# Windowed attention followed by a phase mixer: all x tiles of later batches turned by DMA, theta products split around a channel product

## The chip, the cores and the metric

The kernel runs on one core of a Trainium2 chip. The metric is device time in microseconds (us) of one execution. Five engines with queues of their own work at once: TensorE (PE, matmuls; its weight loads are listed apart as PEld), VectorE (DVE), ScalarE (ACT), GpSimd (POOL) and SyncE (SP, which here only issues DMAs). Each engine takes its instructions in the order in which they were written.

## The reference

Two stages follow each other, for 4 batches, 8 heads, 768 positions and heads of 64 channels (512 channels together).

```
scores = q @ k.T / 8 - slope[h] * dist     # only the 8 first and the 96 last positions are kept
x      = softmax(scores) @ v               # heads side by side: 768 x 512
theta  = x @ w_theta
y      = w_tok_r @ (x * cos(theta)) + w_tok_i @ (x * sin(theta))
u      = x + y
out    = u + max(u @ w_ch, 0)
```

## The kernel before

Positions are cut into six tiles of 128 (`st` or `tt`), channels into four blocks of 128 (`dc`). Heads are worked in pairs, so that a pair's output is one block of 128 channels: pair 0 gives x's channels 0 to 127, pair 3 the last 128.

**Attention of a pair** (`att_transpose`, `att_scores`, `att_values`): q and k are turned on PE into PSUM tiles `ps_tr` (L215) and copied out (L225); scores go in three groups into a wide PSUM tile `ps_w` (L267), ACT takes the exponential (L276), DVE multiplies by a mask (L286, L288), PE multiplies by v into another `ps_w` (L315), and DVE divides by the sums and writes the pair's part of `x_sb` (L322, L323).

**Mixing of a batch**: theta needs x with channels on partitions, `xT`. `turn_x` makes one pair's part of it in one of two ways: six PE transposes into a `ps_tr` tile (L347) and a DVE copy (L352), or one transposing DMA from SBUF to SBUF, issued by SP (L341). `mix_theta(b, st)` then computes theta for two position tiles in one `ps_w` tile: 8 products of 128x128 by 128x512 (L364), after which ACT takes cosine and sine from it (L372, L373). `mix_z` multiplies these by x on DVE (L380, `zri`). `mix_tok` sums twelve products for a position tile in a PSUM tile `ps_mm` (L399), DVE adds x (L404, `u`), and SP issues a transposing DMA of u (L413, `uTd`). `mix_ch` multiplies that by `w_ch` in a `ps_mm` tile (4 products, L441), DVE finishes it (L444), and SP issues the store (L446).

**PSUM.** `ps_w` has two buffers, `ps_mm` two, `ps_tr` two. They are taken in turn, so the next but one user of a kind waits until the readers of the earlier one are done.

**Order.** It is written out by hand. `attend_beside(b + 1, ...)` interleaves attention of batch b + 1 with token products of batch b (`main`, a list of units, taken one or more at a time by `m()`). Then comes the stretch that is changed, in which batch b's last channel products stand between batch b + 1's theta products. It is passed three times, for b + 1 = 1, 2, 3; they are called batches 1, 2 and 3 here. `load` is true in batches 1 and 2, where heads of a further batch are fetched by POOL's DMAs meanwhile (L75, L80). With it, pairs 0 and 1 are turned by DMA, pair 2 on PE ahead of the last units of `main` (L492), pair 3 on PE after a channel product (L586). Batch 3 turns pairs 0, 1 and 2 by DMA and pair 3 on PE. So seven pairs go by DMA and five on PE. Batch 0 has its own order ahead of the loop (L500 to L570) and isn't touched.

In batches 1 and 2, `att_transpose` of the following batch puts its 24 PE transposes between `mix_theta(b + 1, 2)` and `mix_theta(b + 1, 4)`; its copies of k and q stand behind the sines of the latter on ACT and behind `mix_z(b + 1, 2)` on DVE.

Of the kernel before, what the change touches and what calls it, by code (L numbers as in the profile page):

```python
# [16 lines left out]
def kernel(  # L17
# [14 lines left out]
    B, H, S, D = q.shape  # L32
# [3 lines left out]
    NC = DM // T  # L36
# [19 lines left out]
    def ps_wide():  # L56
        return psum.tile([T, 2, DM], FP, name="ps_w", tag="ps_w", bufs=2)

    def ps_acc():
        return psum.tile([T, DM], FP, name="ps_mm", tag="ps_mm", bufs=2)  # L60

    def ps_tr(cols):
        return psum.tile([T, cols], BF, name="ps_tr", tag="ps_tr", bufs=2)
# [20 lines left out]
    def load_heads(b, h0, n):  # L84
        load_qk(b, h0, n)
        load_v(b, h0, n)
# [121 lines left out]
    def att_transpose(b, h0, extras=True, sins=None, q_eng="dve", between=None, cuts=(T,)):  # L208
        pq, pk = ps_tr(S), ps_tr(S)
        for src, pst in ((q_sb[b], pq), (k_sb[b], pk)):  # L210
            if pst is pk and between is not None:
                between()
            for t_ in range(NT):
                for hh in range(2):
                    K(nc.tensor.transpose(pst[hh * D:(hh + 1) * D, t_ * T:(t_ + 1) * T],  # L215
                                          src[:, h0 + hh, t_ * D:(t_ + 1) * D], ident))
        if sins is not None:
            sins()

        kT = abuf.tile([T, S + (NT - 2) * T], BF, name="kT", bufs=2)  # L220
        qT = abuf.tile([T, S], BF, name="qT", bufs=2)
        copy = nc.scalar.copy if q_eng == "act" else nc.vector.tensor_copy
        for op, dst, src in ((nc.scalar.copy, kT[:, 0:S], pk), (copy, qT, pq)):
            for p0, p1 in zip((0,) + cuts, cuts):
                K(op(out=dst.rearrange("a (p t) -> a p t", t=NT)[:, p0:p1, :],  # L225
                     in_=src.rearrange("a (t p) -> a p t", t=NT)[:, p0:p1, :]))
        qTs[b, h0], kTs[b, h0] = qT, kT
        if extras:
            att_extras(b, h0)
# [25 lines left out]
    def att_scores(b, h0, g_):  # L255
        qT, kT = qTs[b, h0], kTs[b, h0]
        blocks = GROUPS[g_]
        n = len(blocks)
        bias = b == 0
        if bias and (h0, g_) not in biased:  # L260
            att_bias(h0, g_)
        ps = biased[h0, g_] if bias else ps_wide()
        for i_, (it, prev) in enumerate(blocks):
            kc = it * T if prev == 0 else (0 if it == 1 else S + (it - 2) * T)
            for hh in range(2):
                R = slice(D * hh, D * (hh + 1))
                K(nc.tensor.matmul(ps[:, hh, i_ * T:(i_ + 1) * T],  # L267
                                   lhsT=kT[R, kc:kc + T], rhs=qT[R, it * T:(it + 1) * T],
                                   start=not bias, stop=not bias or i_ == n - 1))
        if bias:  # L270
            p = abuf.tile([T, 2, 4 * T], BF, name="p", bufs=6)
            K(nc.scalar.activation(p[:, :, 0:n * T], ps[:, :, 0:n * T], AF.Exp, scale=scale))  # L272
            probs[b, h0, g_] = p
            return
        e = abuf.tile([T, 2, 4 * T], BF, name="e", bufs=3)
        K(nc.scalar.activation(e[:, :, 0:n * T], ps[:, :, 0:n * T], AF.Exp, scale=scale))  # L276
        exps[b, h0, g_] = e
        att_mul(b, h0, g_)
# [58 lines left out]
    def turn_x(b, dc, by_dma, eng=nc.vector.tensor_copy):  # L337

        xT = xTs[b][:, dc, :]
        if by_dma:  # L340
            K(nc.sync.dma_start(out=xT.rearrange("a (c t) -> a c t", t=T),  # L341
                                in_=x_sb[b][:, dc, :, :].rearrange("a t d -> a (t d)"),
                                transpose=True))
            return
        pt = ps_tr(S)
        for st in range(NT):
            K(nc.tensor.transpose(pt[:, st * T:(st + 1) * T], x_sb[b][:, dc, st, :], ident))  # L347
        if eng == "both":
            K(nc.vector.tensor_copy(out=xT[:, 0:2 * T], in_=pt[:, 0:2 * T]))  # L349
            K(nc.scalar.copy(out=xT[:, 2 * T:], in_=pt[:, 2 * T:]))  # L350
        else:
            K(eng(out=xT, in_=pt))  # L352
# [3 lines left out]
    def mix_theta(b, st, d0=0, d1=NC):  # L356

        if d0 == 0:
            thetas[b, st] = ps_wide()
        pth = thetas[b, st]  # L360
        for s2 in range(2):
            for dc in range(d0, d1):
                c = (st + s2) * T
                K(nc.tensor.matmul(pth[:, s2, :], lhsT=xTs[b][:, dc, c:c + T],  # L364
                                   rhs=w_theta_bf[:, dc, :],
                                   start=(dc == 0), stop=(dc == NC - 1)))
        if d1 < NC:
            return
        if st == 0:
            zris[b] = mbuf.tile([T, NT, 2, DM], BF, name="zri", tag="zri", bufs=3)  # L370
        cs = mbuf.tile([T, 2, 2, DM], BF, name="cs", bufs=3)
        K(nc.scalar.activation(cs[:, :, 0, :], pth, AF.Sin, bias=halfpi))  # L372
        K(nc.scalar.activation(cs[:, :, 1, :], pth, AF.Sin))  # L373
        css[b, st] = cs

    def mix_z(b, st):
        cs = css[b, st]
        xs = x_sb[b][:, :, st:st + 2, :].rearrange("a c s d -> a s c d")
        for wi in range(2):
            K(nc.vector.tensor_mul(  # L380
                zris[b][:, st:st + 2, wi, :].rearrange("a s (c d) -> a s c d", d=T),
                cs[:, :, wi, :].rearrange("a s (c d) -> a s c d", d=T), xs))
# [49 lines left out]
    def mix_ch(b, tt, parts=1):  # L432
        uT, n, s2 = uTs[b, tt]
        out_t = out[b].rearrange("(t p) d -> p t d", p=T)[:, tt, :]
        N = DM // parts
        for part in range(parts):
            cols = slice(part * N, (part + 1) * N)
            pc = ps_acc()
            for dc in range(NC):
                c = (n * dc + s2) * T  # L440
                K(nc.tensor.matmul(pc[:, 0:N], lhsT=uT[:, c:c + T], rhs=w_ch_bf[:, dc, cols],  # L441
                                   start=(dc == 0), stop=(dc == NC - 1)))
            o_sb = mbuf.tile([T, N], FP, name="o_sb", bufs=4)
            K(nc.vector.scalar_tensor_tensor(o_sb, in0=pc[:, 0:N], scalar=0.0,  # L444
                                             in1=us[b][:, tt, cols], op0=ALU.max, op1=ALU.add))
            K(nc.sync.dma_start(out=out_t[:, cols], in_=o_sb))  # L446
# [24 lines left out]

    def attend_beside(b, main, lead, load):


        def m(n=1):
            for _ in range(n):
                main.pop(0)()

        m(lead)
        for h0 in range(0, H, 2):  # L480
            att_scores(b, h0, 0)
            m()
            att_scores(b, h0, 1)
            att_scores(b, h0, 2)
            if h0 + 2 < H:
                att_transpose(b, h0 + 2, q_eng="act")
                if load and h0 == 0:
                    load_heads(b + 1, 0, 4)
                m(2)
            else:  # L490
                if load:
                    turn_x(b, NC - 2, False)  # L492
                m(len(main) - 1)
            att_values(b, h0)
            if h0 + 2 < H and not (load and h0 + 4 == H):
                turn_x(b, h0 // 2, True)
            m()


# [72 lines left out]
    for b in range(B):  # L572
        if b == B - 1:
            main = tok_units(b, True)
            main.insert(-1, lambda: mix_uT(b, 4, 1, "act"))
            for unit in main:
                unit()
            mix_ch(b, 2)
            mix_ch(b, 3)
            mix_uT(b, 5, 1, "dve")  # L580
            mix_ch(b, 4)
            mix_ch(b, 5, parts=2)
            break
        attend_beside(b + 1, tok_units(b, b > 0), 3 if b else 0, b + 2 < B)
        mix_ch(b, 2)
        turn_x(b + 1, NC - 1, False)  # L586
        mix_ch(b, 3)
        mix_theta(b + 1, 0)
        mix_z(b + 1, 0)
        mix_ch(b, 4)  # L590
        mix_theta(b + 1, 2)
        mix_z(b + 1, 2)
        if b + 2 < B:
            att_transpose(b + 2, 0, sins=lambda: mix_theta(b + 1, 4))
            load_heads(b + 2, 4, 4)
        else:
            mix_theta(b + 1, 4)
        mix_ch(b, 5)
        mix_z(b + 1, 4)
# [35 lines left out]
```

## Time and profile before

| | us |
|---|---|
| median of 3 runs | 175.93 (175.57 to 175.95) |
| the profiled execution | 177.43 |
| its span, first to last instruction | 175.7 |
| what lies around the span | 1.73 |
| PE busy in the span | 165.6 |
| DVE busy | 111.7 |
| ACT busy | 103.8 |
| POOL busy | 60.6 |
| PE transposes of x (L347), 54 of them | 4.5 busy |
| xT by DMA (L341), 7 of them, issue to landing | 2.7 least, 7.1 median, 12.4 most |

Busy time says how long an engine had an instruction in it, and matmuls overlap, so that PE's own figure is not a sum of their lengths: a 128x512 product lasts 380 ns by itself, and eight behind each other take 1.73 us, so 0.216 us each. The timeline lists instructions by their start, with the length, and in brackets how long the engine had stood idle before it and who released it. A row that merges several instructions ("x8") gives the start of the first and the time to the end of the last.

### The profile page before, as it was taken

What the parts mean: (1) busy time and instruction counts of PE and PEld (TensorE: products, weight loads), DVE (VectorE), ACT (ScalarE), POOL (GpSimd) and SP (SyncE); (2) the same over time, 40 slices, a digit from 0 to 9 for tenths busy, and PEclk for the clock granted to TensorE, in tenths of its full rate; (3) what the DMA queues carried; (4) which work ended last, traced back from release to release, by engine and by line L of the source; (5) the groups of instructions that cost most, each with busy time, mean ns of one, the idle gap of its engine ahead of it and who ended that gap; (6) DMA issues with size and microseconds to landing.
All of it is one profiled execution on the core that took longest, in us unless ns stands there. A gap on an engine that the chain in (4) does not pass through costs nothing.

```text
span 175.7 us, 4158 instructions
## 1 busy us (share of the span) xinstructions
PE 165.6 (94%) x1740; PEld 88.1 (50%) x1740; DVE 111.7 (64%) x205; ACT 103.8 (59%) x121; POOL 60.6 (35%) x99
## 2 busy tenths in 40 slices
PE   7889999899999999999998979999999999999992
PEld 2346665566465554445454544546555544444441
DVE  7756654975768784857567691857568784734353
ACT  5697889947777553797846712797756807500010
POOL 8986695004571400049716100049118000000000
PEclk9999999999999999999999999999999999999999
DMA  5999999999999944117999996116999433312325
GB/s 150 185 174 191 212 207 209 191 189 177 131 142 161 193 84 149 63 60 92 174 98 180 153 147 208 63 60 90 174 93 160 104 97 118 119 30 60 90 109 189
DMA packets 57058, 24.05 MB, mean 137 GB/s; under 512 B 43088, under 2 KB 54096, under 8 KB 57040
## 3 DMA queue, kind: packets, MB, share of 16 engines
q0 software_dynamic: 35328, 12.45, 65.8%
q1 hardware_dynamic: 21440, 10.95, 32.0%
q10 hardware_dynamic: 272, 0.39, 0.6%
q8 instruction: 13, 0.21, 0.5%
q14 instruction: 5, 0.04, 0.1%
HBM read 25.69 MB, written 6.29 MB: 182 GB/s over the span
## 4 chain that ended last, share of the span: by engine, by line
PE 56%; DMA 20%; ACT 9%; DVE 7%; POOL 4%; issue 2%; ACTq 0%
PE ps_mm L399 21%; PE ps_mm L441 10%; PE ps_w L364 9%; DMA v_sb<-in_v_dram 7%; DMA uTd<-u 6%; PE ps_tr L215 4%; PE ps_w L267 4%; DMA k_sb<-in_k_dram 4%; PE ps_w L315 3%; ACT kT L225 3%; DMA first<-in_q_dram 3%; ACT cs L373 2%; DVE w_tokT L117 2%; PE ps_w L252 2%; PE ps_mm L315 2%
## 5 line engine op out<-in xcount | busy, mean ns | idle before, releaser
L399 PE MATMUL ps_mm<-zri,w_tokT 128*128 128x512 bf16 x288 | 69.8, 380 | 0.1
L276 ACT ACTIVATE e<-ps_w 128x1024 bf16<-128x1024 f32 (+1 forms) x36 | 33.0, 951 | 19.6 <-PE ps_w L267 19.6
L399 PEld LDWEIGHTS <-w_tokT 128*128 128x128 bf16 x288 | 25.7, 98 | 28.2 <-issue 0.6
L233 POOL COPY kT<-kT 128x512 bf16<-128x512 bf16 x15 | 9.3, 622 | 64.6 <-ACT kT L225 64.6
L372 ACT ACTIVATE cs<-ps_w,halfpi 128x1024 bf16<-128x1024 f32 x12 | 13.4, 1115 | 19.7 <-PE ps_w L364 19.6
L441 PE MATMUL ps_mm<-w_ch_bf,uTd 128*128 128x512 bf16 x88 | 22.6, 380 | 1.4 <-DMA uTd<-u 1.4
L364 PE MATMUL ps_w<-w_theta_bf,xT 128*128 128x512 bf16 x96 | 22.9, 380 | 0.6 <-DVE xT L349 0.4
L404 DVE TENSOR_TENSOR u<-x_sb,ps_mm 128x512 bf16<-128x512 bf16 x24 | 16.2, 681 | 10.5 <-PE ps_mm L399 10.5
L288 DVE TENSOR_TENSOR p<-e,wmask 128x1024 bf16<-128x1024 bf16 x24 | 17.4, 725 | 8.5 <-ACT e L276 8.4
L380 DVE TENSOR_TENSOR zri<-cs,x_sb 128x1024 bf16<-128x1024 bf16 x24 | 16.1, 687 | 9.1 <-ACT cs L372 7.7
L444 DVE SCALAR_TENSOR_TENSOR o_sb<-ps_mm,u 128x512 f32<-128x512 f32 (+1 forms) x25 | 16.6, 664 | 2.8 <-PE ps_mm L441 2.7
L267 PEld LDWEIGHTS <-kT 64*128 64x128 bf16 x352 | 10.0, 94 | 14.7 <-issue 11.0
L267 PE MATMUL ps_w<-qT,kT 64*128 64x128 bf16 x352 | 16.2, 218 | 0.5 <-DVE kT L234 0.5
L225 ACT COPY kT<-ps_tr 128x768 bf16<-128x768 bf16 (+2 forms) x17 | 12.9, 765 | 4.9 <-PE ps_tr L215 4.9
L315 PEld LDWEIGHTS <-p 128*128 128x128 bf16 x352 | 12.9, 97 | 4.5 <-issue 0.8
L364 PEld LDWEIGHTS <-xT 128*128 128x128 bf16 x96 | 8.9, 98 | 11.3 <-DVE xT L349 0.6
L441 PEld LDWEIGHTS <-uTd 128*128 128x128 bf16 x88 | 8.0, 98 | 10.4 <-DMA uTd<-u 1.5
L80 POOL DMA_DIRECT2D v_sb<-in_v_dram x10 | 13.0, 1305 | 0.0
L286 DVE TENSOR_TENSOR p<-e,wmask 128x768 bf16<-128x768 bf16 x12 | 6.7, 559 | 9.9 <-ACT e L276 9.9
L272 ACT ACTIVATE p<-ps_w 128x1024 bf16<-128x1024 f32 (+1 forms) x12 | 11.3, 953 | 1.7 <-PE ps_w L267 1.2
L373 ACT ACTIVATE cs<-ps_w 128x1024 bf16<-128x1024 f32 x12 | 12.2, 1020 | 0.0
L91 POOL COPY v_pv<-v_sb 128x520 bf16<-128x520 bf16 x15 | 9.3, 620 | 8.3 <-DMA v_sb<-in_v_dram 8.3
(80 smaller groups left out, 192.4 us busy)
## 6 DMA issues: line engine op xcount, KB each, us to landing
out_dram<-o_sb SPq DMA_DIRECT2D x23, 256.0 KB, 2.2
q_sb<-in_q_dram POOLq DMA_DIRECT2D x6, 384.0 KB, 8.5
k_sb<-in_k_dram POOLq DMA_DIRECT2D x6, 384.0 KB, 10.1
v_sb<-in_v_dram POOLq DMA_DIRECT2D x6, 384.0 KB, 13.8
w_nat<-in_moe_w_tok_r_dram POOLq DMA_DIRECT2D x1, 1152.0 KB, 12.2
w_nat<-in_moe_w_tok_i_dram POOLq DMA_DIRECT2D x1, 1152.0 KB, 13.4
v_sb<-in_v_dram POOLq DMA_DIRECT2D x4, 192.0 KB, 7.3
q_sb<-in_q_dram POOLq DMA_DIRECT2D x3, 192.0 KB, 6.8
```

Source lines behind the costliest of these rows:

```text
L225: K(op(out=dst.rearrange("a (p t) -> a p t", t=NT)[:, p0:p1, :], in_=src.rearrange("a (t p) -> a p t", t=NT)[:, p0:p1, :]))
L267: K(nc.tensor.matmul(ps[:, hh, i_ * T:(i_ + 1) * T], lhsT=kT[R, kc:kc + T], rhs=qT[R, it * T:(it + 1) * T], start=not bias, stop=not bias ...
L276: K(nc.scalar.activation(e[:, :, 0:n * T], ps[:, :, 0:n * T], AF.Exp, scale=scale))
L288: K(nc.vector.tensor_mul(p.rearrange("a h (r x) -> a h r x", r=2), e.rearrange("a h (r x) -> a h r x", r=2), wmask[:, hs, None, T:3 * T].t ...
L315: K(nc.tensor.matmul(dst, lhsT=lhsT, rhs=rhs, start=(i_ == 0), stop=(i_ == len(mms) - 1)))
L364: K(nc.tensor.matmul(pth[:, s2, :], lhsT=xTs[b][:, dc, c:c + T], rhs=w_theta_bf[:, dc, :], start=(dc == 0), stop=(dc == NC - 1)))
L373: K(nc.scalar.activation(cs[:, :, 1, :], pth, AF.Sin))
L380: K(nc.vector.tensor_mul(zris[b][:, st:st + 2, wi, :].rearrange("a s (c d) -> a s c d", d=T), cs[:, :, wi, :].rearrange("a s (c d) -> a s ...
L399: K(nc.tensor.matmul(acc, lhsT=w_tokT[wi][:, st, tt * T:(tt + 1) * T], rhs=zris[b][:, st, wi, :], start=(done[b, tt] == 0), stop=(done[b, ...
L404: K(nc.vector.tensor_add(us[b][:, tt, :].rearrange("a (c d) -> a c d", d=T), x_sb[b][:, :, tt, :], acc.rearrange("a (c d) -> a c d", d=T)))
L441: K(nc.tensor.matmul(pc[:, 0:N], lhsT=uT[:, c:c + T], rhs=w_ch_bf[:, dc, cols], start=(dc == 0), stop=(dc == NC - 1)))
L444: K(nc.vector.scalar_tensor_tensor(o_sb, in0=pc[:, 0:N], scalar=0.0, in1=us[b][:, tt, cols], op0=ALU.max, op1=ALU.add))
```

## The change

All pairs of batches 1, 2 and 3 are now turned by DMA, so five groups of six PE transposes and their DVE copies go, and five DMAs come, issued by SP straight after the pair's `att_values`. The products of theta are cut in two: for position tiles 0 to 3 those with the first three channel blocks come first (12 products in both `ps_w` tiles), then the channel product `mix_ch(b, 4)`, then the products with the last block (2 and 2), each followed by its sines.

```diff
@@ attend_beside
             else:
-                if load:
-                    turn_x(b, NC - 2, False)
                 m(len(main) - 1)
             att_values(b, h0)
-            if h0 + 2 < H and not (load and h0 + 4 == H):
-                turn_x(b, h0 // 2, True)
+            turn_x(b, h0 // 2, True)
             m()
@@ the loop over batches
         mix_ch(b, 2)
-        turn_x(b + 1, NC - 1, False)
         mix_ch(b, 3)
-        mix_theta(b + 1, 0)
+
+        mix_theta(b + 1, 0, 0, NC - 1)
+        mix_theta(b + 1, 2, 0, NC - 1)
+        mix_ch(b, 4)
+        mix_theta(b + 1, 0, NC - 1, NC)
         mix_z(b + 1, 0)
-        mix_ch(b, 4)
-        mix_theta(b + 1, 2)
+        mix_theta(b + 1, 2, NC - 1, NC)
         mix_z(b + 1, 2)
         if b + 2 < B:
             att_transpose(b + 2, 0, sins=lambda: mix_theta(b + 1, 4))
```

## The prediction

> **What bounds the kernel now.** First the page's busy shares and slices, then the chain of waits, then the timeline around the three stretches that change.
>
> ```profile
> PE 165.6 (94%) x1740; PEld 88.1 (50%) x1740; DVE 111.7 (64%) x205; ACT 103.8 (59%) x121; POOL 60.6 (35%) x99
> ...
> PEclk9999999999999999999999999999999999999999
> DMA  5999999999999944117999996116999433312325
> ```
>
> PE is the bound, at full clock throughout; the DMA engines are full (digit 9) through most of batch 2's attention, and nearly idle in the changed stretches of batches 1 and 3. So what PE loses counts, and so does what PE no longer has to do, but only where PE isn't waiting there anyway. I call the start of batch 1's first theta product T = 66.84; in batches 2 and 3 it is 106.57 and 143.45. Batch 1's stretch, from the timeline:
>
> ```profile
> 66.84 1.89 PE L364 MATMUL ps_w<-w_theta_bf,xT 128*128 128x512 bf16 x8
> 68.57 1.03 PE L441 MATMUL ps_mm<-w_ch_bf,uTd 128*128 128x512 bf16 x4
> 68.77 1.11 ACT L372 ACTIVATE cs<-ps_w,halfpi 128x1024 bf16<-128x1024 f32 x1 [4.81 <-PE ps_w L364]
> 69.78 1.02 ACT L373 ACTIVATE cs<-ps_w 128x1024 bf16<-128x1024 f32 x1
> 69.43 1.89 PE L364 MATMUL ps_w<-w_theta_bf,xT 128*128 128x512 bf16 x8
> 72.05 1.90 PE L364 MATMUL ps_w<-w_theta_bf,xT 128*128 128x512 bf16 x8
> ```
>
> Theta of tiles 0/1 is complete 1.89 us after T; its cosine starts 0.04 later and its sine ends at 70.80. The third theta tile (4/5) takes the buffer that these two read, and starts only at 72.05: 1.25 us to spare.
>
> **Removed: 30 PE transposes, 5 DVE copies.** Six transposes hold PE for 0.34 us (65.64 to 65.98 below), so five groups are 1.7 us at most. I find none of it on the path:
>
> ```profile
> 63.44 0.20 PE L315 MATMUL ps_w<-v_pv,p 128*128 128x65 bf16 x1 [0.16 <-DVE p L288]
> ...
> 65.25 0.68 DVE L404 TENSOR_TENSOR u<-x_sb,ps_mm 128x512 bf16<-128x512 bf16 x1
> 65.64 0.50 PE L347 MATMUL ps_tr<-ident,x_sb 128*128 128x128 bf16 x6
> 65.98 1.02 PE L441 MATMUL ps_mm<-w_ch_bf,uTd 128*128 128x512 bf16 x4
> ```
> ```profile
> 103.82 0.50 PE L347 MATMUL ps_tr<-ident,x_sb 128*128 128x128 bf16 x6
> ...
> 105.69 1.04 PE L441 MATMUL ps_mm<-w_ch_bf,uTd 128*128 128x512 bf16 x4 [1.37 <-DMA uTd<-u]
> ```
>
> - Pair 2, batch 1: PE already waits for the mask product p at 63.44. That ends at 63.38, behind scores that stand ahead of the removed group, so PE comes 0.34 earlier and waits 0.34 longer. Zero.
> - Pair 3, batches 1 and 3: the channel product behind the group, `mix_ch(b, 3)`, needs the `ps_mm` buffer that the addition L404 reads until 65.93 (batch 3: 141.85 + 0.68 = 142.53). It starts at 65.98 and 142.59, 0.05 later: even without the group it can't start earlier. Zero.
> - Batch 2, both pairs: the same product waits until 105.65 for a DMA of u (issued 94.83, landing 10.82 later). Zero; PE waits 0.68 longer.
>
> The DVE copies, 0.55 us each, are followed by DVE waits on ACT and PE; no PE instruction waits for what they delay. Zero.
>
> **Added: five DMAs on SP.** The seven that exist take SP 1.2 to 4.0 us to issue (median 1.3) and land
>
> ```profile
> DMA to landing us min/median/max: 2.7/7.1/12.4
> ```
>
> after that. Pair 3's: x is written at 65.34, 103.52 and 141.94; its first use comes 16 products after T, at 70.30, 110.03 and 146.91, so 4.96, 6.51 and 4.97 us later. In those stretches the queue is quick: the u tile issued at 65.96 landed in 2.4, the one at 104.14 in 3.3. Hidden. Pair 2's in batch 1 (written 59.51, used at 67.3, loads ending near 64) is hidden. In batch 2 it goes out at 97.57, just behind the late u tile, and is used at 107.00. From above: 11.5 us, as the x tile issued at 90.73, lands at 109.07, 2.07 late. From below: the u tile issued behind it (99.10) landed in 7.3, at 106.4, so it is in time. I take zero, since this row is the nearer in time, and keep 2.07 for the range. On SP, behind the new issues: the u tiles of `mix_ch(b, 4)` and `mix_ch(b, 5)` go out 0.7 to 2.5 us later; the first landed 1.9 us before its use in batch 2, and its use moves out by 0.86; the second is used 7.8 us after issue in batch 1, 9.4 in batch 2, 6.9 in batch 3. Stores only leave later. Zero.
>
> The Trainium skill speaks against the change: "VectorE: DVE Perf Modes", section "The three transpose paths", gives 390 ns on TensorE and 1309 ns by DMA for one 128x128 tile, and its rules keep to TensorE where PSUM will do. By its price, as an estimate, six serial TensorE transposes are 2.34 us a group, and five would be worth 11.7 if all were on the path; this trace has 0.34 a group, because they overlap.
>
> **Moved: theta's products.** This is the term that decides. Theta of tiles 0/1 is now complete only after 6 + 6 + 4 + 2 = 18 products instead of 8. The last starts at T + 17 x 0.216 = 3.68 and ends at 4.06; cosine from 4.10, sine from 5.11 to 6.13 (rows above: 1.01 apart, 1.02 long). Only then is the `ps_w` buffer free for tiles 4/5, which PE takes about 0.05 later: T + 6.18. The same wait, seen in batch 0's own order:
>
> ```profile
> 29.89 1.02 ACT L373 ACTIVATE cs<-ps_w 128x1024 bf16<-128x1024 f32 x1
> ...
> 30.95 1.89 PE L364 MATMUL ps_w<-w_theta_bf,xT 128*128 128x512 bf16 x8 [0.16 <-ACT cs L373]
> ```
>
> Sine ends at 30.91, PE goes on at 30.95. Before, tiles 4/5 start at T + 5.21 in batches 1 and 2 (8 + 4 + 8 products and 24 transposes of q and k) and, without those transposes, at T + 4.33 in batch 3 (20 x 0.216). So PE gets waits of **0.97, 0.97 and 1.85 us**. Queued behind them on PE are `mix_ch(b, 5)`, twelve token products and the next scores; all shift. ACT shifts likewise: sines of tiles 2/3 end at T + 8.03, those of 4/5 start at T + 8.11, and the k copy comes at T + 10.02 against 75.90 - 66.84 = 9.06, 0.96 later. POOL's next copies and loads wait for it (a POOL wait of 17.2 us ends so in batch 1), and the chain of waits runs on through them:
>
> ```profile
> 80.31 13.11 DMA v_sb<-in_v_dram
> ...
> 94.83 10.82 DMA uTd<-u
> ```
>
> So batch 1's delay arrives undiminished at batch 2's wait, and batch 2's in batch 3, whose k load ends a PE wait at 125.50. Tail: the twelve-product sums go on without a gap, their last operands from tiles 4/5 having over 1 us to spare as before.
>
> **Sum.** 0.97 + 0.97 + 1.85 = 3.79 us, minus nothing. Profiled execution: 177.43 + 3.79 = 181.2 (span 179.5). It lies 1.5 above the median of runs, so on the median 175.93 + 3.79 = **179.7**.
>
> The 1.37 us wait at 105.69 left PEclk at 9; the longest idle time after the change would be about 2.1 us, in the same place. The Trainium skill, "TensorE: Matmul & The Clock Gate", section "Part 1: The HAM clock gate", halves the clock after an idle window of 3.4 us: by it these waits add nothing; were it to bite once, 3.4 us at half speed would, as an estimate, add 1.7.
>
> **Rivals.**
> - *Late tile in batch 2* (12 in 100). The new x tile is held up by loads. For: 11.5 and 12.4 us of its neighbours. Against: the landing of what is queued behind it. Price up to 2.07: 179.7 to 181.8.
> - *A delay absorbed* (9). DMA traffic, not POOL's issue, sets when batch 2's u tile lands, so batch 1's 0.97 is used up there; or batch 2's before the k load in batch 3. Then 178.8, or 177.8 if both. Against: the loads that fill the queue are themselves issued behind the k copy.
> - *Nothing for nothing* (3). Sines clear the buffer early enough after all, and the transposes were hidden: 175.9. It needs the buffer free by T + 5.21, against my 6.13.
> - *Faster* (6). PE is bound by its own work alone: each removed group gives its 0.34, and tiles 4/5 take a buffer that nobody still reads. 175.93 - 1.70 = 174.2. It decides if the wait at tiles 4/5 is under 0.34 to 0.68 a batch. For: PE's 94%. Against: the row at 30.95, and what ends at 65.93, 142.53 and 105.65.
>
> **Numbers.** Forecast 70 in 100. Its own bounds are 178.8 to 180.7. The range 177.8 to 181.4 takes in the absorbed delays and most of the late tile; 9 in 100 below and some 5 above are left out. A measurement tells about 0.2% from no change; slower by more: 70 + 12 + 9 = 91; within: 3; faster: 6.
>
> **What would show it.** Right: at the third theta tile of each later batch, PE idle 0.97, 0.97 and 1.85 us, released by the sine L373; L364's idle time up from 0.6 to some 4.4 us; the six cosines and sines of a batch with hardly a gap; the wait for uTd in batch 2 grown from 1.37 to about 2.1; PE's busy time down by some 1.7. Wrong: no wait by L373 at L364; theta's last products waiting for xT; `mix_ch(b, 3)` starting under 0.05 us after L404's end; batch 2's u tile landing at an unshifted time.

## The result, and the profile after

The changed kernel takes 184.37 us (median of 6 runs, 182.79 to 185.78) against 176.06 for the kernel before (6 runs): ratio 1.043, 95% interval 1.039 to 1.048. One of the six (185.78) lies over 1.5% above the fastest; such runs are left out of the ratios, here and below. Slower, as forecast, but by 8.3 us at the medians and 7.6 by the ratio and not by 3.8, and above the range. Its runs also spread over 3.0 us where those of before spread over 1.1. The profiled execution took 184.94 us, its span is 183.1, 7.4 more than before. Lines of the page:

```profile
PE 162.5 (89%) x1687; PEld 86.4 (47%) x1710; DVE 109.8 (60%) x200; ACT 103.5 (57%) x121; POOL 61.1 (33%) x99
...
L364 PE MATMUL ps_w<-w_theta_bf,xT 128*128 128x512 bf16 x91 | 22.9, 379 | 5.7 <-ACT cs L373 3.6
...
L441 PE MATMUL ps_mm<-w_ch_bf,uTd 128*128 128x512 bf16 x83 | 21.6, 379 | 3.2 <-DMA uTd<-u 2.2
```

PE's busy time is 3.1 us less (some of it records that are missing: L364 ran 96 times, not 91), and it has 5.7 us of idle time ahead of theta's products, where it had 0.6. Now PE's timeline in batch 1, in batch 2 and in batch 3:

```profile
66.85 2.75 PE L364 MATMUL ps_w<-w_theta_bf,xT 128*128 128x512 bf16 x11
69.44 1.03 PE L441 MATMUL ps_mm<-w_ch_bf,uTd 128*128 128x512 bf16 x4
70.31 1.03 PE L364 MATMUL ps_w<-w_theta_bf,xT 128*128 128x512 bf16 x4
...
73.02 1.89 PE L364 MATMUL ps_w<-w_theta_bf,xT 128*128 128x512 bf16 x8 [0.89 <-ACT cs L373]
```
```profile
107.28 1.04 PE L441 MATMUL ps_mm<-w_ch_bf,uTd 128*128 128x512 bf16 x4 [2.19 <-DMA uTd<-u]
108.15 0.59 PE L364 MATMUL ps_w<-w_theta_bf,xT 128*128 128x512 bf16 x2
110.11 2.33 PE L364 MATMUL ps_w<-w_theta_bf,xT 128*128 128x512 bf16 x9 [1.37 <-DMA xT<-x_sb]
...
115.86 1.89 PE L364 MATMUL ps_w<-w_theta_bf,xT 128*128 128x512 bf16 x8 [0.89 <-ACT cs L373]
```
```profile
148.95 2.75 PE L364 MATMUL ps_w<-w_theta_bf,xT 128*128 128x512 bf16 x11
...
155.12 1.89 PE L364 MATMUL ps_w<-w_theta_bf,xT 128*128 128x512 bf16 x8 [1.69 <-ACT cs L373]
```

The waits for the sine are there in all three batches. In batch 2 stand two more: a longer one for the u tile, and one for pair 2's x tile that the forecast put at zero. The third theta tiles of batches 2 and 3 before (that of batch 3 is the second half of the lower row, so 8 x 0.216 us after its start):

```profile
111.77 1.90 PE L364 MATMUL ps_w<-w_theta_bf,xT 128*128 128x512 bf16 x8
...
146.04 3.62 PE L364 MATMUL ps_w<-w_theta_bf,xT 128*128 128x512 bf16 x16
```

From the starts in these rows and those of before, the lateness grows like this:

| point | before | after | late by | new there |
|---|---|---|---|---|
| third theta tile, batch 1 | 72.05 | 73.02 | 0.97 | 0.97 sine |
| u tile of batch 2 lands | 105.65 | 107.24 | 1.59 | 0.62 loads |
| third theta product, batch 2 | 107.00 | 110.11 | 3.11 | 1.52 x tile |
| third theta tile, batch 2 | 111.77 | 115.86 | 4.09 | 0.98 sine |
| first theta product, batch 3 | 143.45 | 148.95 | 5.50 | 1.41 loads |
| third theta tile, batch 3 | 147.77 | 155.12 | 7.35 | 1.85 sine |
| end of the span | 175.7 | 183.1 | 7.4 | |

So 3.80 us are waits for the sine, 1.52 the x tile, and 2.03 came up between the batches, where the delay was handed on by POOL's loads and grew. Both columns are single executions, that of before 1.4 us above its median, and what hangs on a DMA shifts between executions (in e9 this u tile lands 1.68 us earlier), so the prices of the parts are taken from the runs below. What makes it grow shows on POOL, beside DVE. First the kernel before, in batch 1:

```profile
75.50 1.28 DVE L380 TENSOR_TENSOR zri<-cs,x_sb 128x1024 bf16<-128x1024 bf16 x2
76.76 0.62 POOL L233 COPY kT<-kT 128x512 bf16<-128x512 bf16 x1 [17.20 <-ACT kT L225]
```

Then the changed kernel, POOL in batches 1 and 2, and DVE in batch 1:

```profile
77.72 1.03 POOL L233 COPY kT<-kT 128x512 bf16<-128x512 bf16 x1 [18.14 <-ACT kT L225]
...
120.56 1.03 POOL L233 COPY kT<-kT 128x512 bf16<-128x512 bf16 x1 [21.97 <-ACT kT L225]
```
```profile
76.99 1.28 DVE L380 TENSOR_TENSOR zri<-cs,x_sb 128x1024 bf16<-128x1024 bf16 x2
```

The k copy ahead of the loads lasts 1.03 us in both batches, 0.62 before. It now runs beside the last zri products, which end at 78.27; before, those ended at 76.78, as the copy began. That is 0.4 us of each of the two growths. The rest comes behind the loads: the v load of batch 2 takes 13.5 us to land instead of 13.1, that of batch 3, issued 4.49 us later than before, 13.0 instead of 11.7, and the v copy on POOL that waits for the latter lasts 1.12 us instead of 0.62, again beside a DVE product.

### The profile page after: what moved, and what is told of

Same layout as the page of the kernel before. It is cut to its first block, busy times and chain, and to the rows that moved or that the text cites. A ratio compares the mean times of both kernels' runs of the same rounds, so it can differ in the third digit from the quotient of the medians.

```text
span 183.1 us, 4081 instructions
## 1 busy us (share of the span) xinstructions
PE 162.5 (89%) x1687; PEld 86.4 (47%) x1710; DVE 109.8 (60%) x200; ACT 103.5 (57%) x121; POOL 61.1 (33%) x99
## 4 chain that ended last, share of the span: by engine, by line
PE 50%; DMA 22%; ACT 10%; DVE 7%; POOL 6%; issue 3%; ACTq 0%
PE ps_mm L399 17%; DMA v_sb<-in_v_dram 14%; PE ps_w L364 10%; PE ps_mm L441 7%; DMA xT<-x_sb 5%; PE ps_w L267 3%; PE ps_tr L215 3%; ACT cs L373 3%; PE ps_w L315 3%; ACT kT L225 2%; DMA first<-in_q_dram 2%; ACT cs L372 2%; DVE w_tokT L117 2%; PE ps_w L252 2%; ACT e L276 2%
## 5 line engine op out<-in xcount | busy, mean ns | idle before, releaser
L399 PE MATMUL ps_mm<-zri,w_tokT 128*128 128x512 bf16 x275 | 67.9, 380 | 1.5 <-DVE w_tokT L117 0.5
L233 POOL COPY kT<-kT 128x512 bf16<-128x512 bf16 x15 | 10.1, 670 | 67.1 <-ACT kT L225 67.1
L364 PE MATMUL ps_w<-w_theta_bf,xT 128*128 128x512 bf16 x91 | 22.9, 379 | 5.7 <-ACT cs L373 3.6
L372 ACT ACTIVATE cs<-ps_w,halfpi 128x1024 bf16<-128x1024 f32 x12 | 13.4, 1115 | 25.2 <-PE ps_w L364 24.9
L441 PE MATMUL ps_mm<-w_ch_bf,uTd 128*128 128x512 bf16 x83 | 21.6, 379 | 3.2 <-DMA uTd<-u 2.2
L404 DVE TENSOR_TENSOR u<-x_sb,ps_mm 128x512 bf16<-128x512 bf16 x24 | 16.2, 682 | 10.7 <-PE ps_mm L399 10.7
L288 DVE TENSOR_TENSOR p<-e,wmask 128x1024 bf16<-128x1024 bf16 x24 | 16.6, 692 | 8.1 <-ACT e L276 8.1
L364 PEld LDWEIGHTS <-xT 128*128 128x128 bf16 x96 | 8.9, 97 | 16.6 <-issue 4.0
L91 POOL COPY v_pv<-v_sb 128x520 bf16<-128x520 bf16 x15 | 9.8, 651 | 10.8 <-DMA v_sb<-in_v_dram 10.8
L286 DVE TENSOR_TENSOR p<-e,wmask 128x768 bf16<-128x768 bf16 x12 | 7.3, 606 | 8.8 <-ACT e L276 8.8
## 6 DMA issues: line engine op xcount, KB each, us to landing
w_nat<-in_moe_w_tok_r_dram POOLq DMA_DIRECT2D x1, 1152.0 KB, 11.7
```

Of the source, the lines that this page charges most:

```text
L288: K(nc.vector.tensor_mul(p.rearrange("a h (r x) -> a h r x", r=2), e.rearrange("a h (r x) -> a h r x", r=2), wmask[:, hs, None, T:3 * T].t ...
L399: K(nc.tensor.matmul(acc, lhsT=w_tokT[wi][:, st, tt * T:(tt + 1) * T], rhs=zris[b][:, st, wi, :], start=(done[b, tt] == 0), stop=(done[b, ...
L404: K(nc.vector.tensor_add(us[b][:, tt, :].rearrange("a (c d) -> a c d", d=T), x_sb[b][:, :, tt, :], acc.rearrange("a (c d) -> a c d", d=T)))
```

## The experiments

The theories. **Q**: the third theta tile waits for the sines that still read its PSUM buffer (3.8 us). **P**: DVE work beside POOL's copy lengthens it, and the loads behind it come late against PE. **D2**: pair 2's DMA in batch 2 is late, because loads fill the DMA engines. **Z**: the removed transposes were worth nothing. The rivals were that the DMAs are the whole loss (D in e1), and that the transposes were worth 1.7 us. The theories were worked out from the profile after; each run is compared with the kernel before on the same chip (medians 176.48 for the first four, 175.95 for the next four, 176.02 for the last).

**e1, the order alone.**

```diff
@@ against the kernel before
-        mix_theta(b + 1, 0)
-        mix_z(b + 1, 0)
+        mix_theta(b + 1, 0, 0, NC - 1)
+        mix_theta(b + 1, 2, 0, NC - 1)
         mix_ch(b, 4)
-        mix_theta(b + 1, 2)
+        mix_theta(b + 1, 0, NC - 1, NC)
+        mix_z(b + 1, 0)
+        mix_theta(b + 1, 2, NC - 1, NC)
```

> Only the order of theta's products is changed; x is turned as in the kernel before (five pairs on PE). Theory Q (the third theta tile waits for the sines that still read its PSUM buffer, and this is the larger part of the loss): PE idle at L364 for the sine L373 by 0.97, 0.97 and 1.85 us in batches 1, 2 and 3, no wait for xT, and 0.4 us a batch on top in batches 1 and 2, since POOL's k copy then falls beside DVE's zri products and takes 1.03 instead of 0.62 us: 4.2 to 5.0 us over the kernel before, 180.3 to 181.1. Rival D (the loss comes from the added DMAs): under 2 us over the kernel before, below 178.

Measured 181.99, ratio 1.030 (1.026 to 1.035). The waits for the sine are 0.90, 0.90 and 1.69 of idle time on the page, as in the changed kernel; the k copy lasts 1.03. It is 5.5 over at the medians, a little above what Q with P's 0.4 a batch allowed. Rival D falls: the order is the larger part.

**e2, the DMAs alone**: the changed kernel with theta's products in the order of before.

```diff
@@ against the kernel before, besides the change in attend_beside
         mix_ch(b, 2)
-        turn_x(b + 1, NC - 1, False)
         mix_ch(b, 3)
```

> Only the way of turning x is changed; theta's products stand in the old order, so that the last pair's tile is wanted 3 products after theta starts instead of 16. Theory Q: no wait for the sine at L364. Waits for xT instead: in batches 1 and 3 the tile lands 2.7 us after its issue and is wanted about 2.1 us after it, 0.6 us each; in batch 2 it lands 7.3 us after its issue and is wanted about 4, so 3 to 4 us. Together 4 to 6 us over the kernel before, 180 to 182. Rival (the DMAs cost little by themselves, the order is all): under 2 us over.

Measured 180.46, ratio 1.014 (1.009 to 1.019); single runs lie between 178.8 and 184.1. In the profiled execution, PE waits for xT 0.48 us in batch 1, 0.52 in batch 3 and twice in batch 2, and not for the sine:

```profile
105.87 0.59 PE L364 MATMUL ps_w<-w_theta_bf,xT 128*128 128x512 bf16 x2
108.61 0.39 PE L364 MATMUL ps_w<-w_theta_bf,xT 128*128 128x512 bf16 x1 [2.14 <-DMA xT<-x_sb]
110.85 2.32 PE L364 MATMUL ps_w<-w_theta_bf,xT 128*128 128x512 bf16 x5 [1.85 <-DMA xT<-x_sb]
```

The waits are the ones expected, but this execution is the longest of the four, 184.1 us, and its clock fell (see the last section), so the sizes in batch 2 are not shown for the shorter ones. The time, 4.0 over at the medians and 2.5 by the ratio, is at or below the lower end of what was expected. Either way the DMAs alone cost less than the order alone. The cut of theta's products does what it was made for: in the changed kernel pair 3's tile is never waited for.

**e3, pair 2 back on PE** in batches 1 and 2, all else as changed.

```diff
@@ against the changed kernel
             else:
+                if load:
+                    turn_x(b, NC - 2, False)
                 m(len(main) - 1)
             att_values(b, h0)
-            turn_x(b, h0 // 2, True)
+            if not (load and h0 + 4 == H):
+                turn_x(b, h0 // 2, True)
```

> The changed kernel with pair 2 of batches 1 and 2 turned on PE again (pair 3 by DMA, theta in the new order). Theory D2 (pair 2's DMA in batch 2 is late by itself and also holds up what shares the DMA engines): the wait for xT in batch 2 (1.4 to 1.9 us) goes, the u tile before it lands no later than its loads make it, 1.5 to 2.5 us less than the changed kernel: 181.9 to 182.9. Rival (the DMA engines are simply full, and the wait only moves to the u tile or to v): within 0.7 us of the changed kernel.

Measured 182.49, ratio 1.033 (1.030 to 1.037): about 1.8 us below the changed kernel by the ratios, with some 1 us of uncertainty. In batch 2 the waits for xT and for the u tile are both gone, the three for the sine remain. D2 holds; pair 3's DMA costs nothing that can be told from e1.

**e4, the last channel product ahead of the third theta tile**, so that PE has 0.86 us of work in the wait.

```diff
@@ against the changed kernel
         mix_z(b + 1, 2)
+        mix_ch(b, 5)
         if b + 2 < B:
...
-        mix_ch(b, 5)
         mix_z(b + 1, 4)
```

> The changed kernel with the last channel product (4 products, 0.86 us) put ahead of the third theta tile, into the wait for the sine. Theory Q: that wait shrinks by 0.86 in each batch (0.1, 0.1, 0.9 to 1.0 remain); in batch 3 all of it is gained, in batches 1 and 2 the next batch's k copy still comes at the same time and with it POOL's loads, so nearly nothing is gained there: 0.9 us less than the changed kernel, 183.5. Rival (the wait is not on the path in batch 3 either): no difference. Second rival (PE's own order carries batches 1 and 2, not the loads): 2.6 us less, 181.8.

Measured 183.56, ratio 1.038 (1.030 to 1.047), 0.5% below the changed kernel: the middle expected, but the interval is too wide to exclude the first rival. In the profile the third theta tile still starts at 73.02 in batch 1, now straight behind other work, and the k copy on ACT at 76.86 as in the changed kernel; in batch 3, 0.82 us of idle time for the sine remain of 1.69. The price of the move can't be read from this execution: behind a wait of 1.90 us for k in batch 2 PE's clock fell to 0.50 for some 3.4 us (see the last section), which by itself, as an estimate, costs 1.7.

**e5, e1 with DVE kept off POOL's copy**: the last zri product goes behind the first scores of the next batch.

```diff
@@ against e1
-        mix_z(b + 1, 4)
+        mix_z(b + 1, 4, (0, 1) if b + 2 == B else (0,))
...
             att_scores(b, h0, 0)
             m()
+            if h0 == 0 and late is not None:
+                late()
...
+                      (lambda: mix_z(b, 4, (1,))) if b else None)
```

> The order-only kernel with the last zri product of batches 1 and 2 (DVE, 0.69 us) moved behind the first scores of the next batch, so that DVE does nothing beside POOL's k copy. Theory P (DVE work beside it makes that copy last 1.03 instead of 0.62 us, all loads behind it on POOL go out 0.41 later against PE, and the v load of batch 3 then lands 13 to 14 us after issue instead of 11.7): the copy is back at 0.62, the v load of batch 3 lands within 12.2 us, 1.0 to 1.8 us less than order only: 180.2 to 181.0. Rival (the length of the copy and of the load have other reasons): the copy stays at 1.03, or it shortens and the time stays within 0.5 us of 182.0.

POOL in e1, then in e5:

```profile
77.33 1.03 POOL L233 COPY kT<-kT 128x512 bf16<-128x512 bf16 x1 [18.14 <-ACT kT L225]
...
81.29 1.44 POOL L80 DMA_DIRECT2D v_sb<-in_v_dram  x1
```
```profile
77.33 0.61 POOL L233 COPY kT<-kT 128x512 bf16<-128x512 bf16 x1 [18.14 <-ACT kT L225]
...
80.87 1.44 POOL L80 DMA_DIRECT2D v_sb<-in_v_dram  x1
```

Both copies start at 77.33; without the DVE product beside it, it lasts 0.61, and the load goes out 0.42 earlier. In batch 3 the v load lands 11.5 us after its issue instead of 13.4. Measured 179.63, ratio 1.021 (1.016 to 1.026), some 1.5 us below e1 by the ratios (with 1.2 of uncertainty), 3.8 above the kernel before. P holds in direction, and its size lies within what was expected; what is left of the order's cost is what Q says, 3.8. How a load that goes out 0.4 us later against PE comes to last 1.9 longer isn't shown step by step; in e1 the first transposing DMAs of batch 3 go out 1.57 us after that load and not 2.00, as in e5 and in the kernel before, and the issue of pair 1's tile holds SP for 2.96 us instead of 1.25.

**e6, half the load taken out of batch 2's attention**: heads 2 and 3 of batch 3 are fetched at the end of the iteration.

```diff
@@ against the changed kernel
-                    load_heads(b + 1, 0, 4)
+                    load_heads(b + 1, 0, 4 if b == 1 else 2)
...
+            if b == 1:
+                load_heads(b + 2, 2, 2)
             load_heads(b + 2, 4, 4)
```

> The changed kernel with half of the load that runs beside batch 2's attention (heads 2 and 3 of batch 3) moved to the end of that iteration. Theory D2 (loads that share the DMA engines hold up the u tile and pair 2's tile in batch 2): the waits for uTd (2.2) and xT (1.4) in batch 2 go to under 0.3, its third theta tile starts 3 us earlier than in the changed kernel (115.9), so 112.5 to 113.5; batch 3 pays part of it back where the moved load is wanted early. Rival (DMA transposes are slow in that queue whatever else runs): waits stay above 2 us together, 115 or later.

```profile
105.37 1.02 PE L441 MATMUL ps_mm<-w_ch_bf,uTd 128*128 128x512 bf16 x4 [0.18 <-DVE u L404]
106.23 2.75 PE L364 MATMUL ps_w<-w_theta_bf,xT 128*128 128x512 bf16 x12
...
112.39 1.89 PE L364 MATMUL ps_w<-w_theta_bf,xT 128*128 128x512 bf16 x8 [0.89 <-ACT cs L373]
...
123.17 0.53 PE L215 MATMUL ps_tr<-ident,q_sb 128*64 128x128 bf16 x12 [3.57 <-DMA q_sb<-in_q_dram]
```

The waits for the u tile and for xT in batch 2 are gone, the twelve products run in one piece, and the third theta tile starts at 112.39 instead of 115.86. So the loads are what held the tiles up. As a whole it is no gain: 185.16, ratio 1.052 (1.047 to 1.058), since the moved heads are now waited for in batch 3 (3.57), and PE's clock falls to 0.50 behind that wait.

**e7 and e12, the kernel before with the k copy first; e8, the same on the changed kernel.** The next batch's k copy goes ahead of the last cosine and sine on ACT.

```diff
-            att_transpose(b + 2, 0, sins=lambda: mix_theta(b + 1, 4))
+            att_transpose(b + 2, 0, sins=lambda: mix_theta(b + 1, 4, act=False))
             load_heads(b + 2, 4, 4)
+            mix_sin(b + 1, 4)        # L369 to L374 of the kernel before
```

> The kernel before, with the k copy of the next batch put ahead of the last cosine and sine on ACT. Theory C (POOL's extras and loads, and with them u and v tiles of batches 2 and 3, hang on that copy): copy 2.3 us earlier, loads out 2 us earlier, the waits for v and uTd in batch 2 (1.5 and 1.4 us) and for k and v in batch 3 shrink: 1.5 to 3 us less than the kernel before, 173.5 to 175. Rival (PE's own order carries the time, the loads only fill gaps): within 0.5 us of 176.4.

> The changed kernel with the same move. Theory C: the k copy comes at 8.0 instead of 10.0 us after theta's start, loads 2 us earlier; the delay that batches 1 and 2 hand on through the loads is gone, the waits for the sine on PE itself (0.97, 0.97, 1.85) stay: 2 to 4 us less than the changed kernel, 180.4 to 182.4. Rival: within 0.7 us of 184.4.

> The kernel of e7 once more, on the chip of the run beside it: 1.5 to 3 us less than the kernel before, about 173.8.

e7: 173.79, ratio 0.989 (0.985 to 0.993); e12, the same kernel: 173.78, 0.990 (0.985 to 0.994). In e7's trace PE's matmuls wait for nobody at all from the first theta product of batch 1 to the end. e8: 178.71, ratio 1.014 (1.008 to 1.021), 2.8% below the changed kernel by the ratios, about 5 us where 2 to 4 were expected. So the loads, hung on one copy on ACT, carry the delays of this kernel from batch to batch; with them early, the changed kernel's handed-on delays mostly vanish, while its waits for the sine (0.89 of idle time each in batches 1 and 2, 1.68 in batch 3) and for xT in batch 2 (1.48) are still there. With the copy first in both, the change costs 4.5 us by the ratios (e8 against e7).

**e9, the removed transposes by themselves**: the kernel before without its five groups, and nothing in their place.

```diff
@@ against the kernel before
-                if load:
-                    turn_x(b, NC - 2, False)
...
-        turn_x(b + 1, NC - 1, False)
...
-                K(nc.tensor.matmul(pth[:, s2, :], lhsT=xTs[b][:, dc, c:c + T],
+                K(nc.tensor.matmul(pth[:, s2, :], lhsT=xTs[b][:, dc if b == 0 else (dc % 2 if b < B - 1 else min(dc, NC - 2)),
+                                                 c:c + T],
```

> The kernel before without the five groups of PE transposes and DVE copies, and nothing in their place: theta of batches 1 to 3 uses the channel blocks that went by DMA in their stead, so two blocks of x (one in batch 3) are left out of theta. Theory Z (the removed groups stood beside waits that stay: the mask product, the addition that frees the PSUM tile, the late u tile): within 0.4 us of the kernel before. Rival (PE is bound by its own work, 0.34 us a group): 1.7 us less, 174.3.

Measured 175.77, ratio 0.9996 (0.996 to 1.003), over 12 runs. What stood behind each group waits now:

```profile
63.45 0.20 PE L315 MATMUL ps_w<-v_pv,p 128*128 128x65 bf16 x1 [0.49 <-DVE p L288]
65.99 1.02 PE L442 MATMUL ps_mm<-w_ch_bf,uTd 128*128 128x512 bf16 x4 [0.18 <-DVE u L405]
66.85 1.89 PE L364 MATMUL ps_w<-w_theta_bf,xT 128*128 128x512 bf16 x8
...
104.01 1.04 PE L442 MATMUL ps_mm<-w_ch_bf,uTd 128*128 128x512 bf16 x4 [1.26 <-DMA uTd<-u]
```

The wait for the mask product grows from 0.16 to 0.49, and theta starts at 66.85 as it did at 66.84. In batch 2 the u tile landed 1.68 us earlier than in the profile before, so the cover there can't be read from these two executions. Z holds by the twelve runs: there was nothing to gain, to within some 0.7 us.

**e10 and e11, two ways to cover pair 3's DMA without holding both theta tiles open.** e10 puts `mix_ch(b, 4)` whole ahead of an uncut theta (pair 2 on PE). e11 adds the k copy first, and begins theta's first tile ahead of `mix_ch(b, 3)`.

The stretch in e10, and then in e11, in its order:

```
mix_ch(b, 2)
mix_ch(b, 3)
mix_ch(b, 4)
mix_theta(b + 1, 0)
mix_z(b + 1, 0)
mix_theta(b + 1, 2)
...
```
```
mix_ch(b, 2)
mix_theta(b + 1, 0, 0, NC - 1)
mix_ch(b, 3)
if b + 2 < B:
    mix_ch(b, 4)
mix_theta(b + 1, 0, NC - 1, NC)
mix_z(b + 1, 0)
if b + 2 == B:
    mix_ch(b, 4)
mix_theta(b + 1, 2)
...
```

> Pair 3 by DMA, pair 2 of batches 1 and 2 on PE, and the whole channel product of tile 4 ahead of theta as cover, theta uncut as in the kernel before. Theory Q: theta's first tile is complete 8 products after it starts, so no wait for the sine in batches 1 and 2 and about 0.5 us in batch 3; the tile of pair 3 is wanted 3.6 us after it is written, so no wait in batches 1 and 3 and up to 1 us in batch 2: 0 to 1.5 us over the kernel before, 176 to 177.5. Rival (a DMA for pair 3 costs more than cover can hide): over 178.

> k copy first (as in e7), pair 3 by DMA, and theta's first tile begun ahead of the channel product that waits for the addition, its last two products behind two channel products. If PE is the only bound once the loads are early, up to 0.34 us a batch less than e7: 172.8 to 173.8. If the tile of pair 3 lands late in batch 2, or the sine is waited for: up to 1.5 us more than e7.

e10: 177.85, ratio 1.014 (1.009 to 1.019). The waits at theta are those expected: none for xT, 0.39 for the sine in batch 3. The time is above what was expected, and its cause isn't settled; PE waits 0.97 for POOL's v copy in batch 2 and 0.42 for a u tile in batch 3, in which a v copy of POOL lasts 1.12 us beside DVE. e11: 173.57, ratio 0.988 (0.985 to 0.992), not to be told from e12 (173.78) beside it. The best kernels here are thus the one before with the k copy moved, and e11.

## Why the prediction was wrong

- **Bound, and the removed transposes at zero**: right, by e9 to within 0.4%. All three covers named are in the traces: p, the addition L404 (idle 0.18 ahead of `mix_ch(b, 3)`), and the u tile. That its wait came out at 2.19 where some 2.1 was forecast is partly luck: the tile landed 0.62 later than forecast, and PE came to it later too, by about 0.5.
- **The moved products**: right in mechanism and size. T + 6.18 was forecast for the third theta tile; it starts at T + 6.17 in batches 1 and 3. Forecast 0.97, 0.97 and 1.85 us; the starts give 0.97, 0.98 and 1.85.
- **Added DMAs, pair 3**: right; never waited for in the changed kernel.
- **Added DMAs, pair 2 in batch 2**: wrong. "I take zero, since this row is the nearer in time" chose between 0 and 2.07; it was 1.52. Issued at 100.03, the tile landed 10.0 us later, at 110.07, 2.8 us behind the u tile ahead of it. The row it was taken from, a u tile that landed at 106.4, was of a queue without this tile in it, and landed when the loads had just ended (the last at 106.0). In the changed kernel they had not: the loads went out 1.4 us later, the last landed at 110.5, and the u tile ahead went out 2.8 later. The other row, 11.5 us for the x tile of pair 1, was of the same kind of transfer under load, and was the one to choose. The late tile was a rival with 12 in 100.
- **"Batch 1's delay arrives undiminished"**: this is the larger of the two steps that failed, and with the waits for the sine it is enough to pass the range (175.93 + 3.79 + 2.03 = 181.75). The delay did not pass on one to one; it grew by 0.62 and then 1.41 us. No rival had a delay that grows. The sum let every engine's work shift together, and so did not ask what would now stand beside what: the zri products on DVE hang on the sines, the k copy on ACT too, but the POOL copy behind it came to stand beside the last product. e5 shows this cause, with about 1.5 us by the ratios, in the kernel with the order alone; in the changed kernel 0.4 us a batch is read from the copy itself, and how the loads turn it into 2.03 is not shown step by step.
- **Sum**: 3.79 forecast. By the table 3.80 + 1.52 + 2.03 = 7.35 in the profiled executions; by the ratios of the runs, 3.8 for the order (e5), 1.5 for POOL and the loads (e1 less e5), 1.8 for pair 2 (after less e3), 7.1 of 7.6 (4.3% of 176.06), the last two with some 1 us of uncertainty each.
- **Range**: its upper end took in most of one added loss and nothing for a handed-on delay that grows, though the chain it leaned on runs through loads under a full DMA queue, and these took 13.5 and 13.0 us where they had taken 13.1 and 11.7.

## What to carry to other kernels

Before work is taken off a bound engine, look at what the next instruction on it waits for: if that ends when the removed work ended, nothing is gained. Splitting an accumulation to cover a late operand keeps its PSUM buffer for longer, so count the products to the last one, add the readers, and compare with the buffer's next user. When a delay is handed on, check which instructions of other engines come to stand beside each other, and price a transfer under load by its like under load.

## What the runs showed of the hardware

A POOL copy and a DVE product with two SBUF inputs slow each other down. The copy of 0.62 us lasts 1.03 when the product has started first. In the kernel before, the reverse: a mask product of 0.69 us that starts at 93.53, just behind a POOL copy (93.47), lasts 1.10. The Trainium skill, "SBUF — State Buffer", section "SBUF: two separate sides", has DVE and GpSimd share one pair of ports as an exclusive lock, held for the whole instruction; these rows agree: the copy ends 0.48 us after the product, most of the 0.62 that it takes alone.

Turning a tile by DMA costs PE no instructions, but its landing goes with the load: 2.7 us at best, 7.3 to 14.4 in batch 2 of the changed kernel (pairs 2 and 3: 10.0 and 7.3, and with half the load, in e6, 5.3 and 2.8), and SP was held up to 5.25 us by the issue of one (1.2 in a quiet queue).

PE's clock fell to half after waits that were each short, and no one length decides it. In e2's profiled execution PE waits 2.14 us from 106.46, runs one product at 108.61 and waits again; in e4's it waits once, 1.90 us from 86.64 to 88.54. The view by windows (us, length, busy time of PE, PEld, DVE, ACT and POOL, granted clock, DMA share, GB/s), e2 and then e4:

```profile
108.00:108.50 0.50, 0.00 (x0) 0.00 (x0) 0.00 (x0) 0.00 (x0) 0.00 (x0) 1.00 1.20 193
108.50:109.00 0.50, 0.39 (x1) 0.10 (x1) 0.00 (x0) 0.00 (x0) 0.00 (x0) 0.88 1.01 336
109.00:109.50 0.50, 0.00 (x0) 0.00 (x0) 0.00 (x0) 0.00 (x0) 0.00 (x0) 0.50 1.57 287
```
```profile
88.00:88.50 0.50, 0.00 (x0) 0.00 (x0) 0.50 (x1) 0.00 (x0) 0.13 (x1) 1.00 1.47 121
88.50:89.00 0.50, 0.46 (x10) 0.46 (x12) 0.17 (x1) 0.00 (x0) 0.00 (x0) 0.51 1.85 154
```

In e2 the clock is at half by 109.0, as the first wait's product ends, and stays there until about 115.7; four channel products then took 1.91 us instead of 1.03. In e4 it is at half as the single wait ends, until about 91.9. Yet in e6 it was still at 1.00 when a wait of 3.57 us ended at 123.17, and fell about 1 us later; and in the changed kernel's profiled execution the waits of 2.19 and 1.37, with six products between them, left it at 1.00 (the five other runs of it had means of 0.989 to 1.000). The prediction cited the Trainium skill, "TensorE: Matmul & The Clock Gate", for an idle window of 3.4 us, by which waits of 2 us add nothing; e4's single wait of 1.90 us differs from that, and the measurement decides.
